# A new two-dimensional FFT (radix-4/2 over d, 128-point transforms over s, a t transform with ±f unpacking) under a scheduler with buffer pools

## The chip, the cores and the metric

The kernel runs on one core of a Trainium2 chip. Times are device microseconds (us) of one execution, and medians over several. Most executions agree within a per cent (in b1's batch, 9 of the 11 of the unchanged kernel lay within 1% of their median). A run is marked slow when it lies more than 1.5% above the fastest of the same kernel. "Span" is the profiled length of one execution, about 2 us shorter than its time. Engines: PE is TensorE (PEld its weight loads), DVE VectorE, ACT ScalarE, POOL GpSimd, SP SyncE, which issues most transfers. Nothing here uses more than one core.

## The reference, cut to what matters

Two paths read the same x (2048 rows s, 512 columns d) and are mixed by a gate for each row.

```python
def _A_ref(x, w_r, w_i):                       # x: 1 x 2048 x 512
    X = rfft2(x.astype(float32), axes=(-2, -1))    # 2048 x 257, complex
    X = X * (w_r + 1j * w_i)
    return irfft2(X, s=(S, D)).astype(bfloat16)
def _B_ref(x, w1, b1, w2):
    h = einsum("bsd,df->bsf", x, w1) + b1          # 512 -> 1792
    act = h * tanh(softplus(h))
    return einsum("bsf,fd->bsd", act, w2)
g = sigmoid((x * gate_w).sum(-1, keepdims=True))
return g * _A_ref(...) + (1 - g) * _B_ref(...)
```

## The kernel before

Both FFT directions are written as matmuls with constant matrices: a transform over d (a1), one over part of s (s1), a round trip through DRAM scratch that turns the data so that the rest of s lies on the partitions, a second transform there (s2), the multiplication by W, and the same way back (s2i, scratch, s1i, a1i). The two large matmuls of path B (mm1 and mm2) fill TensorE's gaps. A list scheduler orders all tasks on each engine before the kernel is emitted.

The d transform makes half-width products (64 output partitions each), 16 matmuls of 256 columns for each of the 16 tiles:

```python
def f_a1(e, t=t, bank=bank):
    for bx in range(2):
        for dt_ in range(4):
            for c in range(2):
                ins = e.matmul(ps[64 * c:64 * c + 64, bank, 256 * bx:256 * (bx + 1)],
                               xT[:, dt_, t, bx:128:2],
                               FD_sb[:, dt_, 256 * c:256 * (c + 1)], ...)
```

The result of s1 is evicted (copied by ACT or DVE out of ps, TensorE's output in PSUM) into one of **two** staging tiles, each stored to scratch after four tiles; the third group of four waits for the first store:

```python
T2 = sb("T2", [128, 2, 4, 512], BF)
Y1s = [T2[:, i, :, :].rearrange("p g (h k) -> p (g h) k", h=2) for i in range(2)]
...
def f_e2(e, t=t, sbank=sbank):
    return e.activation(Y1s[(t // 4) % 2][:, (t % 4)::4, :], ps[:, sbank, :]..., AF.Copy)
if t % 4 == 3:
    ...dma(f"r1w{gi}_{bx}", scr1_w[:, b0:b0 + 4, :], Y1s[gi % 2][:, 4 * bx:4 * bx + 4, :], ...)
```

W is loaded by GpSimd's queue, one transfer for the real and one for the imaginary part. Each row is read twice, so that each transfer fills all 128 partitions with 16,448 contiguous bytes:

```python
Wrv = A_w_r.rearrange("(j g) k -> j (g k)", g=32).unsqueeze(1).to_broadcast([64, 2, 32 * 257])
t_wr = dma("ld_wr", WaT[:].rearrange("p g k -> p (g k)"), Wrv, ..., queue="pool", deps=t_w1)
```

Of the kernel before, what the change touches and what calls it, by code (L numbers as in the profile page):

```python
# [8 lines left out]
BF = mybir.dt.bfloat16  # L9
# [5 lines left out]
NT = 16  # L15
NFT = 14
NCH = 4

# [8 lines left out]
def _q_of(c, e):  # L27
    return 64 * c + e


def _build_consts():
    cs = {}
    d = np.arange(D, dtype=np.float64)[:, None]
    k = np.arange(256, dtype=np.float64)[None, :]
    ang = 2 * np.pi * d * k / D
    FD = np.zeros((D, 512))
    FD[:, :256] = np.cos(ang)
    FD[:, 256:] = -np.sin(ang)
    FD[:, 256] = (-1.0) ** np.arange(D)
    cs["FD"] = FD.reshape(4, 128, 512).transpose(1, 0, 2)  # L40
    n = np.arange(D, dtype=np.float64)[None, :]
    kk = np.arange(256, dtype=np.float64)[:, None]
    ang2 = 2 * np.pi * kk * n / D
    GD = np.zeros((512, D))
    GD[:256, :] = 2 * np.cos(ang2)
    GD[256:, :] = -2 * np.sin(ang2)
    GD[0, :] = 1.0
    GD[256, :] = (-1.0) ** np.arange(D)
    GD /= (S * D)
    cs["GD"] = GD.reshape(2, 2, 128, D).transpose(2, 1, 0, 3).reshape(128, 4, D)  # L50
    a = np.arange(64, dtype=np.float64)[:, None]
    e = np.arange(64, dtype=np.float64)[None, :]
    qre = np.array([_q_of(0, ee) for ee in range(64)])
    qim = np.array([_q_of(1, ee) for ee in range(64)])
    M1 = np.zeros((128, 32, 128))
    G1 = np.zeros((128, 32, 128))
    for b in range(32):
        th = -2 * np.pi * e * (32 * a + b) / S
        c_, s_ = np.cos(th), np.sin(th)
        M1[0:64, b, qre] = c_  # L60
        M1[64:128, b, qre] = -s_
        M1[0:64, b, qim] = s_
        M1[64:128, b, qim] = c_
        thi = (2 * np.pi * e * (32 * a + b) / S).T
        ci, si = np.cos(thi), np.sin(thi)
        G1[qre, b, 0:64] = ci
        G1[qim, b, 0:64] = -si
        G1[qre, b, 64:128] = si
        G1[qim, b, 64:128] = ci
    cs["M1"] = M1  # L70
    cs["G1"] = G1
    RF = np.zeros((128, 128))
    RI1 = np.zeros((128, 128))
    for b in range(32):
        for dd in range(32):
            ph = -2 * np.pi * b * dd / 32
            fw = [[np.cos(ph), np.sin(ph)], [-np.sin(ph), np.cos(ph)]]
            iv = [[np.cos(ph), -np.sin(ph)], [np.sin(ph), np.cos(ph)]]
            for m2 in range(2):
                for ci_ in range(2):  # L80
                    for co in range(2):
                        RF[4 * b + 2 * ci_ + m2, 4 * dd + 2 * m2 + co] = fw[ci_][co]
                        RI1[4 * dd + 2 * m2 + co, 4 * b + 2 * ci_ + m2] = iv[co][ci_]
    RI2 = RI1[np.arange(128) ^ 1, :]
    P1k = np.zeros((128, 128))
    P0k = np.zeros((128, 128))
    Jm = np.zeros((128, 128))
    for dd in range(32):
        for m2 in range(2):
            for co in range(2):  # L90
                po = 4 * dd + 2 * m2 + co
                P1k[4 * (31 - dd) + 2 * (1 - m2) + co, po] = 1
                if m2 == 1:
                    P0k[4 * (31 - dd) + 2 + co, po] = 1
                else:
                    P0k[4 * ((32 - dd) % 32) + co, po] = 1
                Jm[po ^ 1, po] = 1
    small = np.stack([RF, RI1, RI2, P0k, P1k, Jm], axis=1)
    cs["SMALL"] = small
    cs["SGN"] = np.where(np.arange(128) % 2 == 0, 1.0, -1.0).astype(np.float32).reshape(128, 1)  # L100
    return cs


class _Task:
    __slots__ = ("name", "eng", "dur", "fn", "deps", "lat", "sem", "semval", "idx", "sig",
                 "start", "done", "succ", "bl", "prio", "xfer", "ninst", "opts", "isdma")

    def __init__(self, name, eng, dur, fn, lat=0.0, prio=0.0):
        self.name = name
        self.eng = eng  # L110
        self.dur = dur
        self.fn = fn
        self.deps = []
        self.lat = lat
        self.sem = None
        self.semval = 0
        self.idx = -1
        self.sig = 0
        self.start = 0.0
        self.done = 0.0  # L120
        self.succ = []
        self.bl = 0.0
        self.prio = prio
        self.xfer = 0.0
        self.ninst = 0
        self.opts = None
        self.isdma = False


OPT_BIAS = {"act": 0.0}  # L130
SCH = dict(eps=0.1, sync=0.1)


class _Cnt:
    def __init__(self, e):
        self._e = e
        self.n = 0

    def __getattr__(self, k):
        f = getattr(self._e, k)  # L140

        def w(*a, **kw):
            self.n += 1
            return f(*a, **kw)  # L144

        return w


class _Graph:
    ENGS = ("pe", "act", "dve", "pool", "sp")  # L150

    def __init__(self):
        self.tasks = []
        self.last_w = {}
        self.readers = {}
        self.cur_prio = 0.0
        self.win_first = None
        self.win_last = None

    def add(self, name, eng, dur, fn, reads=(), writes=(), lat=0.0, deps=(), prio=None):  # L160
        if prio is None:
            prio = self.cur_prio
        t = _Task(name, eng, dur, fn, lat, prio)
        dset = []
        seen = set()

        def _add(d):
            if d is not None and d is not t and id(d) not in seen:
                seen.add(id(d))
                dset.append(d)  # L170

        for d in deps:
            _add(d)
        for r in reads:
            _add(self.last_w.get(r))
        for w in writes:
            _add(self.last_w.get(w))
            for rd in self.readers.get(w, ()):
                _add(rd)
        for r in reads:  # L180
            self.readers.setdefault(r, []).append(t)
        for w in writes:
            self.readers[w] = []
            self.last_w[w] = t
        t.deps = dset
        t.idx = len(self.tasks)
        self.tasks.append(t)
        return t

    def add_multi(self, name, opts, reads=(), writes=(), deps=(), prio=None):  # L190
        e0, d0, f0 = opts[0]
        t = self.add(name, e0, min(o[1] for o in opts), f0, reads=reads, writes=writes, deps=deps, prio=prio)
        t.opts = list(opts)
        return t

    def schedule(self):
        tasks = self.tasks
        for t in tasks:
            t.succ = []
            t.start = -1.0  # L200
# [3 lines left out]
        for t in reversed(tasks):  # L204
            m = 0.0
            for s_ in t.succ:
                if s_.bl > m:
                    m = s_.bl
            t.bl = t.dur + t.lat + m
        nleft = {id(t): len(t.deps) for t in tasks}  # L210
        ready = [t for t in tasks if not t.deps]
        free = {e: 0.0 for e in self.ENGS}
        order = {e: [] for e in self.ENGS}
        nsched = 0
        EPS = SCH['eps']
        SYNC_LAT = SCH['sync']
        dq_free = 0.0
        dq2_free = 0.0
        while nsched < len(tasks):
            best = None  # L220
            best_est = None
            ests = []
            for t in ready:
                if t.opts is None:
                    est = free[t.eng]
                    for d in t.deps:
                        dd = d.done + (0.0 if d.eng == t.eng else SYNC_LAT)
                        if dd > est:
                            est = dd
                else:  # L230
                    bo = None
                    for (oe, od, of) in t.opts:
                        e_ = free[oe]
                        for d in t.deps:
                            dd = d.done + (0.0 if d.eng == oe else SYNC_LAT)
                            if dd > e_:
                                e_ = dd
                        sc = e_ + od + (OPT_BIAS.get(oe, 0.0) if (self.win_first is not None and self.win_first.start >= 0 and self.win_last.start < 0) else 0.0)
                        if bo is None or sc < bo[0] - 1e-9:
                            bo = (sc, e_, oe, od, of)  # L240
                    est = bo[1]
                    t.eng, t.dur, t.fn = bo[2], bo[3], bo[4]
                ests.append((est, t))
                if best_est is None or est < best_est:
                    best_est = est
            best = None
# [666 lines left out]
```

## Time and profile before

The first three runs had a median of 179.32 us (177.5 to 179.56).

| From the profile before (span 176.1 us) | us |
|---|---|
| TensorE busy | 156.0 |
| of it mm1 and mm2 | 53.1 + 50.2 |
| of it the d transform forward (a1), back (a1i) | 18.6, 15.3 |
| longest idle stretch of TensorE (from 32.6 us) | 8.9 |
| stage t (s2, W, s2i) starts | 73.4 |
| from TensorE's last matmul to the end | 5.6 |

These lines are from the page of the kernel before: busy time and share of each engine, then the span in 40 equal slices (a digit is the busy share in tenths, PEclk the granted TensorE clock in tenths, GB/s what the transfers moved).

```profile
span 176.1 us, 2584 instructions
PE 156.0 (89%) x1032; PEld 78.8 (45%) x1047; DVE 67.2 (38%) x117; ACT 67.1 (38%) x112; POOL 19.3 (11%) x47
...
PE   1798997405999999999999999999999999999990
...
PEclk9999999975999999999999999999999999999997
DMA  5999199993003594800113020286013010101101
GB/s 170 298 415 387 30 323 433 370 381 108 4 0 117 174 280 135 372 0 0 58 63 123 0 119 4 119 270 207 0 64 116 4 60 0 63 0 60 51 9 60
```

TensorE is nearly full except in the first slices and in a hole from the eighth to the tenth. Just before and in it (slices seven to nine) the transfers run at 370 to 433 GB/s.

The groups of instructions, by line, engine, operation and tiles (busy us, mean ns; then idle time just before and what ended it), and the transfers (KB each, median us to landing):

```profile
L144 PE MATMUL ps<-fdgd,xT 128*64 128x256 bf16 x256 | 18.6, 294 | 1.3 <-DMA fdgd<-c_fd 1.2
L144 ACT ACTIVATE T<-ps 128x512 bf16<-128x512 f32 x13 | 7.7, 598 | 16.6 <-DMA scr<-T 10.1
...
WaT<-in_A_w_r_dram POOLq DMA_DIRECT2D x1, 2056.0 KB, 8.7
WbT<-in_A_w_i_dram POOLq DMA_DIRECT2D x1, 2056.0 KB, 13.3
```

The hole is explained by the second line: ACT waits 10.1 us for the store of a staging tile, and TensorE for ACT. The view of the chain that ended last shows the store, and the timeline of TensorE the hole (start, length, instruction, and in brackets the idle time before it):

```profile
21.74 18.41 DMA scr<-T
...
41.49 8.76 PE L144 MATMUL ps<-xT,w_sb 128*128 128x512 bf16 x31 [8.88 <-ACT hsreg L144]
```

**Two modes.** In later batches two executions of this unchanged kernel took 167.0 and 167.3 us at a mean granted clock of 0.999. The other 40 of 42 took 176.8 to 182.9. All profiles of it are of the longer kind. Where one of the two stood in a batch, its neighbours near 180 us were marked slow by the 1.5% rule, so I don't use the ratios of those two batches and compare medians of the changed kernels instead.

### The profile page before, as it was taken

Reading aid. Unit: us, or ns where it says so; the run is one execution under the profiler, and the core shown is the slowest. Engines: PE = TensorE matmul, PEld = TensorE weight load, DVE = VectorE, ACT = ScalarE, POOL = GpSimd, SP = SyncE. Lnnn points to the kernel's source line nnn. Section 1 sums busy time; section 2 is a strip of 40 time slices with the busy share of each in tenths; the row PEclk is TensorE's granted clock in tenths of the full one; section 3 lists DMA queues with packets and bytes.
Section 4 is the critical chain, followed back from the end, with each engine's and each line's share of the span. In section 5 each row is a group of like instructions: output and inputs, shape, how many; then the busy total and the mean of one; then the engine's idle time right before and its main releaser. Section 6 shows DMA issues by size and latency. Waiting matters only on the chain.

```text
span 176.1 us, 2584 instructions
## 1 busy us (share of the span) xinstructions
PE 156.0 (89%) x1032; PEld 78.8 (45%) x1047; DVE 67.2 (38%) x117; ACT 67.1 (38%) x112; POOL 19.3 (11%) x47
## 2 busy tenths in 40 slices
PE   1798997405999999999999999999999999999990
PEld 0676673202367433344444444435555554444440
DVE  0133523000015300245577877400856635160624
ACT  2154637006674677668442186163311230300000
POOL 1000250099100040012000000000000000000000
PEclk9999999975999999999999999999999999999997
DMA  5999199993003594800113020286013010101101
GB/s 170 298 415 387 30 323 433 370 381 108 4 0 117 174 280 135 372 0 0 58 63 123 0 119 4 119 270 207 0 64 116 4 60 0 63 0 60 51 9 60
DMA packets 13856, 23.97 MB, mean 136 GB/s; under 512 B 853, under 2 KB 10325, under 8 KB 13077
## 3 DMA queue, kind: packets, MB, share of 16 engines
q1 hardware_dynamic: 13076, 17.77, 29.3%
q0 software_dynamic: 768, 6.05, 8.7%
q8 instruction: 8, 0.13, 0.3%
q14 instruction: 4, 0.02, 0.1%
HBM read 17.52 MB, written 6.29 MB: 135 GB/s over the span
## 4 chain that ended last, share of the span: by engine, by line
PE 80%; DMA 13%; DVE 3%; issue 1%; SPq 1%; ACT 1%; ACTq 0%
PE ps L144 80%; DMA scr<-T 10%; DMA hsreg<-in_A_x_dram 3%; DVE bs L144 2%; DVE xT L144 1%; SPq L144 1%; DVE T L144 0%; ACT T L144 0%; ACT hsreg L144 0%; ACTq L831 0%; SPq L831 0%
## 5 line engine op out<-in xcount | busy, mean ns | idle before, releaser
L144 PE MATMUL ps<-xT,w_sb 128*128 128x512 bf16 x218 | 53.1, 388 | 10.4 <-ACT hsreg L144 10.0
L144 PE MATMUL ps<-w_sb,hsreg 128*128 128x512 bf16 x216 | 50.2, 379 | 0.4
L144 ACT ACTIVATE hsreg<-ps,b1f 128x512 bf16<-128x512 f32 x56 | 38.1, 688 | 22.2 <-PE ps L144 22.0
L144 PEld LDWEIGHTS ps<-xT,w_sb 128*128 128x128 bf16 x224 | 19.6, 99 | 39.6 <-ACT hsreg L144 20.4
L144 PEld LDWEIGHTS ps<-w_sb,hsreg 128*128 128x128 bf16 x224 | 21.6, 98 | 24.6
L144 DVE CAST T<-ps 128x512 bf16<-128x512 f32 x19 | 13.0, 691 | 37.5 <-PE ps L144 37.3
L144 DVE TENSOR_SCALAR bs<-ps,omg 128x512 bf16<-128x512 f32 x15 | 11.3, 751 | 29.7 <-PE ps L144 21.5
L144 PE MATMUL ps<-fdgd,xT 128*64 128x256 bf16 x256 | 18.6, 294 | 1.3 <-DMA fdgd<-c_fd 1.2
L144 ACT ACTIVATE TT<-ps 128x256 bf16<-128x256 f32 x18 | 6.9, 452 | 25.3 <-PE ps L144 25.2
L144 PEld LDWEIGHTS ps<-fdgd,xT 128*64 128x64 bf16 x256 | 14.0, 117 | 4.5 <-issue 1.9
L144 DVE TENSOR_TENSOR bs<-ps,WaT 128x512 bf16<-128x512 f32 x16 | 10.3, 685 | 13.5 <-PE ps L144 13.5
L144 ACT ACTIVATE Abuf<-ps 128x512 bf16<-128x512 f32 x16 | 9.6, 598 | 15.3 <-PE ps L144 15.3
L144 PE MATMUL ps<-fdgd,TT 128*128 128x512 bf16 x64 | 15.3, 379 | 0.0
L144 ACT ACTIVATE T<-ps 128x512 bf16<-128x512 f32 x13 | 7.7, 598 | 16.6 <-DMA scr<-T 10.1
L144 DVE SCALAR_TENSOR_TENSOR bs<-ps,gcol,bs 128x512 bf16<-128x512 f32 x16 | 12.0, 751 | 3.7 <-PE ps L144 2.8
L144 DVE COPY xT<-ps 128x512 bf16<-128x512 bf16 x13 | 5.3, 423 | 14.4 <-PE ps L144 14.4
L144 DVE TENSOR_TENSOR bs<-ps,WbT 128x512 bf16<-128x512 f32 x16 | 10.2, 682 | 0.0
L144 PEld LDWEIGHTS ps<-fdgd,TT 128*128 128x128 bf16 x64 | 6.3, 98 | 7.6
L144 PE MATMUL ps<-identt,hsreg 128*128 128x128 bf16 x64 | 6.0, 238 | 3.9 <-DMA hsreg<-in_A_x_dram 3.4
L144 PE MATMUL ps<-bs,sm 128*128 128x512 bf16 x32 | 8.4, 379 | 0.0
L144 POOL TENSOR_SCALAR WbT<-WbT,sgnf 128x8224 bf16<-128x8224 bf16 x1 | 7.1, 7122 | 0.1
L144 PEld LDWEIGHTS ps<-identt,hsreg 128*128 128x128 bf16 x64 | 4.1, 106 | 5.9 <-DMA hsreg<-in_A_x_dram 3.8
(53 smaller groups left out, 57.1 us busy)
## 6 DMA issues: line engine op xcount, KB each, us to landing
WaT<-in_A_w_r_dram POOLq DMA_DIRECT2D x1, 2056.0 KB, 8.7
WbT<-in_A_w_i_dram POOLq DMA_DIRECT2D x1, 2056.0 KB, 13.3
scr<-T SPq DMA_DIRECT2D x8, 256.0 KB, 8.8
Abuf<-scr SPq DMA_DIRECT2D x2, 1024.0 KB, 5.9
scr<-T SPq DMA_DIRECT2D x4, 512.0 KB, 2.6
Abuf<-scr SPq DMA_DIRECT2D x4, 512.0 KB, 5.4
out_dram<-bs SPq DMA_DIRECT2D x8, 256.0 KB, 2.0
w_sb<-in_B_w_dram SPq DMA_DIRECT2D x2, 896.0 KB, 12.3
```

Of the source, the lines that this page charges most:

```text
L144: return f(*a, **kw)
```

## The change

The intent: less TensorE work in the FFT, no waits on shared staging, and one scheduler that also gives out buffers. The d transform becomes a radix-4/2 step: additions and subtractions on DVE and GpSimd first, then matmuls of full width. The way back makes half the columns and unfolds them in the last element-wise step. All 16 staged tiles have their own place. The t transform unpacks frequencies +f and −f together, for which the mirrored half of W has to lie on partitions 32 to 63 and 96 to 127 in reverse order. So W is loaded in pieces: 32 neighbouring partitions in long rows, and 16 partitions (every second one) in 514-byte rows written backward. They go on SP's queue, among the scratch stores. PSUM banks and small tiles come from pools at scheduling time. The whole diff is some 1,600 lines; its core (cuts marked):

```diff
-                for bx in range(2):
-                    for dt_ in range(4):
-                        for c in range(2):
-                            ins = e.matmul(ps[64 * c:64 * c + 64, bank, 256 * bx:256 * (bx + 1)], ...)
+                ff = mk("d", XB[:, 2:4, tr_, :], xT[:, 0:2, tr_, :], xT[:, 2:4, tr_, :], ALU.subtract)
+                ff = mk("s", xss, xT[:, 0:2, tr_, :], xT[:, 2:4, tr_, :], ALU.add)
+                ...  # two more of half the size
+                e.matmul(o[:, :, 2:4, :], XB[:, 2, t, :], f4(256), start=True, stop=False)
+                e.matmul(o[:, :, 2:4, :], XB[:, 3, t, :], f4(512), start=False, stop=True)
+                e.matmul(o[:, :, 0, :], XB[:, 0, t, :], f2(0), start=True, stop=True)
+                return e.matmul(o[:, :, 1, :], XB[:, 1, t, :], f2(128), start=True, stop=True)
 ...
-        T2 = sb("T2", [128, 2, 4, 512], BF)
+        A1s = R4[:].rearrange("p (t k) -> p t k", t=NT)
 ...
-        t_wr = dma("ld_wr", WaT[:].rearrange("p g k -> p (g k)"), Wrv, ..., queue="pool", deps=t_w1)
+                v = src_t.rearrange("(g h e2 j) k -> g h e2 j k", g=16, h=2, e2=2)
+                wl.append(dma(f"ld_{nm}p{co}", dst[base:base + 32, :, :].rearrange("p j k -> p (j k)"),
+                              v[:, 0, :, :, :].rearrange("g e2 j k -> g e2 (j k)"), 32 * 16448, ...))
+                nb = dst[base + 32:base + 64, :, :]
+                def back(part, j, npart, nj, pstep):
+                    return bass.AP(nb.tensor, nb.offset + part * row + j * 257, [[pstep * row, npart], [-257, nj], [1, 257]])
+                n1 = bass.AP(src_t.tensor, src_t.offset + 65 * 257, [[128 * 257, 16], [257, 32], [1, 257]])
+                wl.append(dma(f"ld_{nm}r{co}", back(0, 31, 16, 32, 2), n1, 16 * 32 * 514, ...))
+                ...  # 31 more such rows for the odd partitions, and one row for each of 16 partitions
 ...
+        fpool = _Pool(4)
+        mpool = _Pool(4)
```

Here `base` is 0 or 64. W's bytes don't change (4.2 MB).

## The prediction

> **What bounds the kernel now.** The chain that ended last is 80% TensorE and 13% DMA; TensorE is busy 156.0 of 176.1 us (page, parts 1 and 4). The timeline of TensorE shows its 20 us of idle time: 3.0 at the start, 8.9 at 32.6-41.5 us (waiting for ACT, which itself waited 10.1 us to reuse the staging tile T, whose store had an 18.4 us DMA piece in the chain), 5.6 after the last matmul, small gaps elsewhere. The kernel is bound by TensorE work plus one DMA stall. DVE and ACT (38% each) have slack on average.
>
> **What the change removes on TensorE.** (groups by shape)
> - d transform forward: 256 half-width matmuls of 256 columns, 18.6 us, become per tile two of 256 and two of 128 columns at full width. Estimate from s1 (5.5 us/32 at 256 columns, part of it overlap; about 0.11-0.12 each) and s1i (4.9/64 at 128 columns): about 6 us. Saves 12.5.
> - d transform back: 64 matmuls of 512 columns, 15.3 us, become 64 of 256: about 7.5. Saves 7.8.
> - s and t matmuls, mm1 (53.1) and mm2 (50.2) stay. TensorE falls to about 134-136 us.
>
> **What it adds or moves.**
> - Butterflies: 32 SBUF add/subtracts (23 on DVE, 9 on GpSimd by the order listing). [...]
> - Front stage: 16 transposes plus 32 full evictions (0.60 ACT, 0.69 DVE) plus butterflies make about 18 us on ACT and 21 on DVE. The front becomes eviction-bound: it should end near 29 us (the first transform now ends at 57.6).
> - All 16 staged tiles have their own place, so the 8.9 us stall goes.
> - W weights: the same 4.1 MB, now hardware queue, half of it in 514-byte rows, queued among scratch writes. About 11.8 MB precede the scratch reads; at the 370 GB/s of the busy slices that lands near 34 us, so stage t starts at about 39-41 us (now 73.4).
> - Stage t: each gp has four 256-wide multiplies instead of two 512-wide. The 256-wide casts start 0.335 us apart, the 512-wide multiplies 0.60: 1.28 becomes about 1.5 us per gp, 26-29 us with its share of evictions. TensorE has about 31 us there. Near balance: 32-34 us.
> - Final stage: DVE gets three instructions a tile (0.75 + 2x0.45) instead of one; still about 26 us under 36 us of TensorE work. The end is 8 last output adds hidden under mm2, tail about 3.3 us instead of 5.6.
>
> **Sum.** Front and its wait to 40; stage t to 73; mm2/mm1 filler 9 us while scratch 2 goes round, to 82; remaining TensorE work (64 s1i, 64 a1i, 92 mm1, 168 mm2) 69 us plus 1-2 of waits, to 152.5; tail to 156 span. Run time is 2 us above the span here. Prediction 157.5 us, range 151 to 167 (from 179.3). Faster 0.95, same 0.03, slower 0.02.
>
> **What would show it right.** TensorE busy 133-138 us; a1 group 5-7 us, a1i 7-8; no gap over 4 us after about 32 us; idle time concentrated before 40 us; the chain's DMA share falling, DVE/ACT share rising in the front; 256-wide multiplies at 0.42-0.45 us.
>
> **What would make it wrong.** 514-byte rows slow, so that W and scratch reads land after 45 us; the front's in-order DVE/ACT/GpSimd waits stretching it past 34 us, with TensorE's granted clock dropping in the gaps (0.975 mean now; the first stage already ran at half speed: 1.92 against 1.07 us a tile); strided W reads or self-waits making stage t DVE-bound (over 36 us).

The sum of the forecast is a span of 156 us, a time of 157.5 (range 151 to 167). The sum itself starts at 40 us, where the transfers put stage t's start, and comes to 157.5.

## The result, and the profile after

The changed kernel took 168.0 us median (166.5 to 169.2, four runs, one of them marked slow) against 179.4 (177.5 to 179.8, four runs). The ratio of the fast runs is 0.935, 95% interval 0.924 to 0.946: faster, but by 11 us where 22 were predicted, and just outside the range. A ratio here is the mean time of one kernel's fast runs over that of the other's of the same rounds, so it isn't quite the ratio of the medians. Repeated on another chip, the changed kernel took 168.3 us (r1 below).

The page of the changed kernel, the same parts:

```profile
span 164.8 us, 2256 instructions
PE 137.2 (83%) x835; PEld 72.3 (44%) x850; DVE 74.5 (45%) x172; ACT 76.4 (46%) x126; POOL 9.3 (6%) x16
...
PE   1397998693002999999999999999999999999991
...
PEclk9999999999655699999999999999999999999999
DMA  4798999999999993030303891100101000011011
GB/s 144 282 374 336 248 157 342 153 280 139 344 135 282 385 354 118 38 127 0 127 0 142 242 258 64 64 4 0 64 0 66 4 0 0 0 64 64 4 64 64
...
L687 PE MATMUL ps<-Wa,SM 128*128 128x32 bf16 x1 | 0.2, 217 | 13.9 <-DMA Wb<-in_A_w_i_dram 13.9
...
L851 PE MATMUL ps<-GD,TT 128*128 128x256 bf16 x64 | 9.1, 273 | 0.0
...
Wa<-in_A_w_r_dram SPq DMA_DIRECT2D x2, 514.0 KB, 9.5
Wb<-in_A_w_i_dram SPq DMA_DIRECT2D x2, 514.0 KB, 11.2
```

TensorE's work fell by 18.8 us (156.0 to 137.2), nearly as predicted (20 to 22). The span fell by 11.3 only, because TensorE's idle time (span less busy) rose from 20.1 to 27.6 us. The old 8.9 us hole is gone and a new one of 13.9 us stands in slices 10 to 13. A transfer ended it: the first matmul that reads W (L687, which prepares a small table) waited for W's imaginary part. The GB/s line shows what differs: in the fifth to thirteenth slices it swings between about 140 and 340, while the DMA digits say 9. The engines read as busy and move little.

The timeline of TensorE around the hole:

```profile
28.49 0.82 PE L637 MATMUL ps<-R,FT 128*128 128x512 bf16 x2 [0.36 <-ACT R L505]
30.70 7.94 PE L785 MATMUL ps<-xT,w_sb 128*128 128x512 bf16 x36 [1.39 <-ACT hsb L793]
52.54 0.22 PE L687 MATMUL ps<-Wa,SM 128*128 128x32 bf16 x1 [13.89 <-DMA Wb<-in_A_w_i_dram]
...
53.21 0.39 PE L733 MATMUL ps<-R,SM 128*128 128x256 bf16 x1 [0.19 <-DMA R<-scr]
```

The front ends at 29.3 us, as predicted; TensorE then takes the mm1 work that fits, and stands still from 38.6 to 52.5. Stage t starts at 53.2 instead of the predicted 39 to 41. SP's queue shows why the scratch reads (R<-scr) came as late as W:

```profile
20.34 7.72 SPq L480 DMA_DIRECT2D Wa<-in_A_w_r_dram  x4
28.23 0.47 SPq L480 DMA_DIRECT2D scr<-R  x1
28.74 6.41 SPq L480 DMA_DIRECT2D Wb<-in_A_w_i_dram  x4
35.68 0.34 SPq L480 DMA_DIRECT2D FT<-c_gt  x1
36.18 0.36 SPq L480 DMA_DIRECT2D scr<-R  x1
36.59 7.71 SPq L480 DMA_DIRECT2D Wb<-in_A_w_i_dram  x4
45.83 1.81 SPq L480 DMA_DIRECT2D R<-scr  x4
```

To issue four W pieces took SP 6.4 to 7.7 us here, and 3.3 us for the first four, at 15.84; what held SP is not shown. The last scratch store was issued at 36.18, and the reads that wait for it only at 45.83: the store, behind three quarters of W, took 9.57 us. The chain that ended last has both (start, length):

```profile
36.18 9.57 DMA scr<-R
45.83 7.33 DMA R<-scr
```

The table by stretches (us from:to and length; busy us of PE, PEld, DVE, ACT, POOL; granted clock; DMA share; GB/s), changed kernel:

```profile
29.30:38.60 9.30, 7.91 (x37) 3.45 (x36) 0.99 (x3) 8.31 (x13) 0.00 (x0) 1.00 1.08 194
38.60:52.50 13.90, 0.04 (x1) 0.00 (x0) 0.00 (x0) 0.69 (x1) 0.00 (x0) 0.64 1.15 221
52.50:85.90 33.40, 32.80 (x158) 15.24 (x163) 24.69 (x72) 17.45 (x29) 0.00 (x0) 0.95 0.42 155
85.90:161.50 75.60, 75.12 (x420) 38.63 (x427) 29.10 (x56) 31.75 (x51) 0.00 (x0) 1.00 0.19 60
```

Between 29.3 and 52.5 us the transfers ran at 194 and 221 GB/s with a share above 1. After the hole, all went as predicted or slightly better. So the question is narrow: why do 4.2 MB of W, which the kernel before loaded without TensorE waiting for it, take so long here?

### The profile page after: what moved, and what is told of

Same layout as the page of the kernel before. It is cut to its first block, busy times and chain, and to the rows that moved or that the text cites. A ratio compares the mean times of both kernels' runs of the same rounds, so it can differ in the third digit from the quotient of the medians.

```text
span 164.8 us, 2256 instructions
## 1 busy us (share of the span) xinstructions
PE 137.2 (83%) x835; PEld 72.3 (44%) x850; DVE 74.5 (45%) x172; ACT 76.4 (46%) x126; POOL 9.3 (6%) x16
## 3 DMA queue, kind: packets, MB, share of 16 engines
HBM read 16.34 MB, written 6.29 MB: 137 GB/s over the span
## 4 chain that ended last, share of the span: by engine, by line
PE 76%; DMA 13%; ACT 4%; POOL 2%; issue 1%; SPq 1%; DVE 0%; POOLq 0%
PE ps L803 29%; PE ps L785 28%; DMA scr<-R 6%; DMA R<-scr 4%; PE ps L851 4%; DMA R<-in_A_x_dram 3%; PE ps L832 2%; PE ps L759 2%; PE ps L760 2%; PE ps L735 2%; PE ps L582 2%; ACT R L505 2%; POOL PX L602 1%; PE ps L659 1%; PE ps L637 1%
## 5 line engine op out<-in xcount | busy, mean ns | idle before, releaser
L793 ACT ACTIVATE hsb<-ps,b1f 128x512 bf16<-128x512 f32 x56 | 37.9, 688 | 30.5 <-PE ps L785 30.1
L803 PE MATMUL ps<-w_sb,hsb 128*128 128x512 bf16 x218 | 49.7, 379 | 0.3
L803 PEld LDWEIGHTS ps<-w_sb,hsb 128*128 128x128 bf16 x224 | 21.8, 98 | 25.5
L505 ACT ACTIVATE R<-ps 128x512 bf16<-128x512 f32 (+1 forms) x29 | 16.8, 594 | 7.7 <-PE ps L760 5.0
L504 DVE CAST R<-ps 128x512 bf16<-128x512 f32 (+1 forms) x19 | 12.8, 689 | 9.1 <-PE ps L760 6.2
L746 DVE TENSOR_TENSOR PX<-ps,Wa 128x256 bf16<-128x256 f32 x32 | 12.0, 416 | 0.6 <-PE ps L734 0.6
L746 DVE TENSOR_TENSOR PX<-ps,Wb 128x256 bf16<-128x256 f32 x32 | 12.0, 417 | 0.1
L687 PE MATMUL ps<-Wa,SM 128*128 128x32 bf16 x1 | 0.2, 217 | 13.9 <-DMA Wb<-in_A_w_i_dram 13.9
L851 PE MATMUL ps<-GD,TT 128*128 128x256 bf16 x64 | 9.1, 273 | 0.0
L874 DVE SCALAR_TENSOR_TENSOR R<-ps,gcol,PX 128x256 bf16<-128x256 f32 x16 | 7.7, 482 | 1.2 <-ACT PX L865 0.8
L875 DVE SCALAR_TENSOR_TENSOR R<-ps,ngcol,PX 128x256 bf16<-128x256 f32 x16 | 7.6, 476 | 0.0
## 6 DMA issues: line engine op xcount, KB each, us to landing
w_sb<-in_B_w_dram SPq DMA_DIRECT2D x4, 896.0 KB, 11.8
```

What stands on the lines that cost most here:

```text
L504: G.add(name, [("dve", dve_dur(n), lambda e: e.tensor_copy(out=outf(), in_=inf())), ("act", act_dur(n), lambda e: e.activation(outf(), inf ...
L505: ("act", act_dur(n), lambda e: e.activation(outf(), inf(), AF.Copy))],
L746: ins = e.tensor_tensor(out=po, in0=px, in1=pw, op=ALU.mult)
L793: return e.activation(hsb[:, hb, ft, :], ps[:, bk(sl), :], AF.Mish, bias=b1f[:, ft:ft + 1])
L803: ins = e.matmul(ps[:, bk(sl), :], hsb[:, hb, ft, 128 * tl:128 * (tl + 1)], w2_sb[:, ft, :], start=(ft == 0), stop=(ft == NFT - 1))
L851: ins = e.matmul(ps[:, bk(sy), 256 * hh:256 * (hh + 1)], TT[:, st.i, i, :], GD[:, i, :], start=(i % 2 == 0), stop=(i % 2 == 1))
```

## The experiments

Three theories. **Rows:** half of W now goes in 514-byte rows, slow each. **Queue order:** W stands between the scratch stores on SP's queue; on another queue it would not hold them up. **Spread:** a transfer to few partitions (narrowness), or to partitions that lie close together, is slow whatever its rows. The change's W pieces all lie within 0 to 63 or 64 to 127, where those of the kernel before filled all 128. Twelve kernels ran.

### m1: the row shapes by themselves

A kernel that only loads, two transfers of each kind and a wait (its result is wrong).

```diff
+ a: rows(16 partitions, every 2nd of 32..63) x 32 rows of 514 B, backward     # the kernel's own
+ c: 512 B of each row, rows 514 B apart in SBUF;  d: 512 B rows 512 B apart in SBUF
+ h: 16 partitions as in a, 16448 B contiguous;    i: 32 neighbours x 16448 B
+ j: 128 partitions x 2056 B contiguous;           k: as a, but 16 neighbouring partitions
```

> Measures the disputed cost by itself (the result is wrong on purpose): fourteen kinds of load into SBUF, each two transfers of about 263 KB in one queue, one kind after the other with a wait between. The mirrored half of a weight in the changed kernel goes as 16 partitions x 32 backward rows of 514 B, and the trace shows about 140 GB/s while they run. Row theory (short rows of 514 B are what is slow): 514 B rows take about 1.9 us per 263 KB more than the fixed time wherever they go (16 or 128 partitions, forward or backward), 16 KB rows into the same 16 partitions about 0.7 us. Narrowness theory (few partitions are what is slow): 16 KB rows into 16 or 32 partitions are as slow as 514 B rows, and 514 B rows into 128 partitions are fast. [...]

It ran once, 89.5 us. From one kind's issue to the next's: a 6.22, c 6.06, d 4.82, h 4.74, i 7.12, j 3.34, k 9.86 us. All moved 0.53 MB except i, 1.05 MB. Part of each is fixed: 128 full partitions took 3.34 us for 0.53 MB here and 4.72 for 1.05 MB in m2, so I estimate 1.96 us fixed and 1.38 us per 0.53 MB. Less that, short rows cost 4.26 us against 2.78 in the same 16 partitions (a against h, a factor of 1.5), and those 16 partitions cost 2.78 against 1.38 of all 128 (h against j, a factor of 2). With k, 16 neighbours, the short rows were slower again: 7.9 us. Rows matter, and so does which partitions they go to, which the rows theory has no place for. The direction and the place of the rows in the source mattered little (forward rows 6.05 us against a's 6.22; d, with its source rows 514 bytes apart, 4.82, and with source rows 1,024 bytes apart 4.75). In these 16 partitions the 512-byte rows of d are about as fast as the long rows of h (4.82 against 4.74 us), while the same rows laid 514 bytes apart (c) took 6.06, so there the place of the rows in SBUF cost more than their length. Less the fixed part, d gains a factor of 1.5 over a (4.26 to 2.86 us).

Two more kinds of this run speak against narrowness alone: 514-byte rows spread over all 128 partitions, four to each (f), took 5.42 us, and 512-byte rows laid 512 bytes apart and spread so (g) 4.30, against j's 3.34. Less the fixed part, f costs 3.46 us against j's 1.38: short rows stay slow on all partitions, and spreading them gained less (4.26 to 3.46) than spreading long ones.

### e1: long rows, same partitions

```diff
-                n1 = bass.AP(src_t.tensor, ..., [[128 * 257, 16], [257, 32], [1, 257]])
-                wl.append(dma(f"ld_{nm}r{co}", back(0, 31, 16, 32, 2), n1, ...
+                lrow = lambda part, ln: bass.AP(nb.tensor, nb.offset + part * row, [[2 * row, 16], [1, ln]])
+                n1 = bass.AP(src_t.tensor, ..., [[128 * 257, 16], [1, 32 * 257]])
+                wl.append(dma(f"ld_{nm}r{co}", lrow(0, 32 * 257), n1, ...
```

The mirrored half is no longer mirrored, so the result is wrong; bytes, partitions and engine order stay.

> The changed kernel with the mirrored half of both weights loaded forward in rows of 16 KB into the same 16 partitions, by the same number of transfers at the same place in the queue (wrong result on purpose; the instruction order of every engine is the same). Row theory: 2.07 MB at about 390 instead of 140 GB/s saves about 9.4 us of DMA time ahead of the scratch reads; the 13.9 us wait of TensorE before the first table matmul shrinks to about 4 us, time about 158 us (156 to 161). Narrowness theory and queue-order theory (scratch transfers held back behind the weights in one queue, whatever their rows): 166 to 168 us, no change.

163.0 us (162.2 to 163.5, four fast runs). The wait before the table's matmul fell to 10.2 us:

```profile
PE ps L687 <- DMA Wb<-in_A_w_i_dram: 10.2, 1, 10.2
```

The row theory expected about 158. It got 5 us of the 10: rows are a part, not the main cause.

### e2: W on another queue

```diff
                 wl.append(dma(f"ld_{nm}p{co}", ...,
-                              writes=[(o, co, 0)], deps=wdep))
+                              writes=[(o, co, 0)], deps=wdep, queue="pool"))
```

and the same for the other three pieces; the result is right.

> The changed kernel with the 16 weight loads, rows unchanged, issued from the GpSimd queue, so that scratch stores and reads no longer stand behind them in the SyncE queue; all instructions of TensorE, ACT and DVE in the same order. Queue-order theory: the fourth scratch store is issued at about 30.5 us instead of 36.2, its reads land near 42, time falls by 6 to 10 us (158 to 162). Row theory: the DMA engines are full until 52 us whichever queue feeds them, the last weight still lands near 50, time 165 to 169.

170.7 us (170.5 to 172.3, four fast runs): no faster than the changed kernel, if anything slower (1.6%, from another batch). The waits of TensorE show the trade:

```profile
PE ps L687 <- DMA Wb<-in_A_w_i_dram: 8.4, 1, 8.4
...
PE ps L733 <- DMA R<-scr: 7.6, 1, 7.6
```

W came earlier, the scratch reads later, and the sum of the two (16.0 us) is worse than 13.9 + 0.2. Order only chose who waits. W was no faster by this queue: in slices 6 to 11 of this run's page the transfers move 176 to 206 GB/s while the DMA digits say 9. The queue theory falls.

### f1: a first repair, long rows and a reversal on chip

The mirrored half lands in long rows in a staging tile, and DVE and GpSimd copy it in reverse order.

```diff
+        Wst = hsb[:, 1:3, :, :]...                      # mm1's output buffer, still unused
+        lrow = lambda part, ln: bass.AP(nb.tensor, ..., [[2 * row, 16], [1, ln]])
+        def f_rev(e, ...): return e.tensor_copy(out=dst[base + 32:base + 64, ...], in_=nb[:, 31 - 16 * hh:...:-1, :])
+        G.add(f"rev_{nm}{co}{hh}", [("dve", REV_DVE, f_rev), ("pool", REV_POOL, f_rev)], ...)
```

> A repair with the right result: the mirrored halves are loaded forward in 16 KB rows into the still unused part of the activation buffer, and DVE and GpSimd, which idle from 30 to 52 us, copy them with the rows reversed (eight copies of 32 x 4112 elements; at GpSimd's 0.87 ns an element of the first kernel about 3.7 us each[...]). Row theory: time 156 to 162, better than both kernels, stage t starting near 40 to 44 us. Queue-order and narrowness theories: 166 us or more.

163.5 us (162.7 to 164.5, four fast runs), right, and no better than e1: its last reversing copies could only start at 49.9 us, when the last staging transfer had landed. It also made a new wait. The timelines of GpSimd and DVE:

```profile
27.58 7.43 POOL L574 COPY Wa<-hsb 32x4112 bf16<-32x4112 bf16 x2 [4.05 <-DMA hsb<-in_A_w_r_dram]
```

```profile
27.63 3.91 DVE L609 TENSOR_TENSOR R<-PX 128x256 bf16<-128x256 bf16 x2
...
35.16 1.24 DVE L574 COPY Wa<-hsb 32x4112 bf16<-32x4112 bf16 x1
```

A copy took 1.24 us on DVE and 3.6 to 4.7 on GpSimd, and while GpSimd copied, two DVE additions that take 0.31 us each in the changed kernel took 3.91 together. Why is not shown; the later repairs use DVE alone.

### m2: the partitions by themselves

```diff
+ a: 128 partitions x 4112 B        b: 64 neighbours x 8224 B     c: every 2nd of 128, 64 x 8224 B
+ d: 32 neighbours x 16448 B        e: every 2nd of 64, 32        f: every 4th of 128, 32 x 16448 B
+ g: 16 neighbours x 16448 B        h: every 8th of 128, 16 x 16448 B
+ i..l: every 4th, 32 x 32 rows of 514 B, 514/528/544/576 B apart
```

> The transfers by themselves again, now two of 526 KB per kind (wrong result on purpose). In the first such run 16 neighbouring partitions moved 66 GB/s and 16 alternate ones 136 with the same 514 B rows, and 32 neighbouring partitions with 16 KB rows about 206 against about 390 for 128 partitions. [...] 64 neighbouring partitions are no faster than 32 (about 206 GB/s), 32 alternate partitions of the first 64 the same, every fourth of 128 partitions fast (350 or more), 64 alternate ones of 128 fast, 16 neighbours about 105, every eighth about 206. Partition-count theory: speed follows the number of partitions: 64 twice 32, every fourth as slow as 32 neighbours. [...]

Issues of SP, start and length; what matters is the distance from one start to the next. Shown are the starts of a, b and c, then of f and g:

```profile
9.02 0.85 SPq L40 DMA_DIRECT2D dst<-in_A_w_r_dram  x2
13.74 1.14 SPq L42 DMA_DIRECT2D dst<-in_A_w_r_dram  x2
21.00 1.13 SPq L44 DMA_DIRECT2D dst<-in_A_w_r_dram  x2
...
40.37 1.12 SPq L50 DMA_DIRECT2D dst<-in_A_w_r_dram  x2
45.67 0.78 SPq L52 DMA_DIRECT2D dst<-in_A_w_r_dram  x2
```

| kind | partitions | us | GB/s (estimate, 1.96 us taken off) |
|---|---|---|---|
| a | 128 | 4.72 | 381 |
| c | every 2nd, 64 | 5.06 | 340 |
| f | every 4th, 32 | 5.30 | 315 |
| b | 64 neighbours | 7.26 | 199 |
| d | 32 neighbours | 6.99 | 209 |
| e | every 2nd of 64, 32 | 7.32 | 196 |
| h (half the bytes) | every 8th, 16 | 4.68 | 193 |
| g (half the bytes) | 16 neighbours | 6.71 | 111 |

The number of partitions does not decide: 32 spread ones (f, 315 GB/s) are faster than 64 neighbours (b, 199). The rates fall into three groups: all, every second and every fourth of the 128 partitions run at 315 to 381 GB/s; 64 or 32 neighbours, every second of 64 and every eighth of 128 at 193 to 209; 16 neighbours at 111. So within the first 64 partitions, 64 gave no more than 32 (b and d), and over all 128 every fourth sufficed for most of the rate, though f stayed below the 350 expected, while every eighth (h) did not suffice. Why the groups lie so is not shown. The short rows i to l, on every fourth of 128 partitions, took 6.12 to 6.29 us at every spacing, about 250 GB/s, against about 123 for m1's kind a in 16 of 32 partitions (0.53 MB in 4.26 us). So a wider spacing did not help. Spread alone doesn't set the rate of short rows: m1's f, on all 128 partitions, makes only about 152 (0.53 MB in 3.46 us), which stays unexplained. This ran once, 95.7 us, with a wrong result.

### e3: the same bytes to all partitions

```diff
-                wl.append(dma(f"ld_{nm}p{co}", dst[base:base + 32, :, :]..., 32 * 16448, ...
-                ... (the pieces r, n, s)
+                for i, (nr, ch) in enumerate(((8, "p"), (4, "r"), (3, "n"), (1, "s"))):
+                    sv = bass.AP(src_t.tensor, ..., [[32 * 257, 64], [0, 2], [1, nr * 257]])
+                    wl.append(dma(f"ld_{nm}{ch}{co}", dst[:, r0:r0 + nr, :]..., sv, 128 * nr * 514, ...
```

As many transfers and bytes, the order of every engine unchanged; the result is wrong.

> The changed kernel with the same number of weight transfers of the same bytes in the same places of the queue, but each to all 128 partitions with rows of 0.5 to 4 KB (wrong result on purpose; order on every engine unchanged). [...] 4.2 MB at about 370 GB/s instead of about 165 saves about 13 us of DMA time: the wait before the table matmul falls from 13.9 us to under 2, time 154 to 158 us. If the queue's order or the total of bytes were the cause: 161 us or more, as with long rows alone (163.0).

156.1 us (155.4 to 157.3, four fast runs). The wait and the same stretches:

```profile
PE ps L687 <- DMA Wb<-in_A_w_i_dram: 1.8, 1, 1.8
```

```profile
29.30:38.60 9.30, 7.91 (x37) 3.44 (x36) 1.11 (x3) 8.41 (x13) 0.00 (x0) 1.00 1.03 363
38.60:52.50 13.90, 10.81 (x52) 5.04 (x53) 6.85 (x22) 5.08 (x9) 0.00 (x0) 0.75 0.92 307
```

The rate from 29.3 to 38.6 us rose from 194 to 363 GB/s at about the same DMA share (1.08 and 1.03), and the kernel became 11.9 us faster. The spread theory's expectation holds (154 to 158 us). e3 alone changes spread, number of partitions and row length together, and reads each source row twice, as the kernel before did. m2 tells these apart for the transfers: 64 neighbouring partitions gained nothing over 32 (b, 199 GB/s, against d, 209), and its kind a, which reads every byte once, still ran at 381 GB/s.

### e4: all partitions, short rows

```diff
+            for i, (nr, ch) in enumerate(((8, "p"), (4, "r"), (3, "n"), (1, "s"))):
+                dv = bass.AP(dst..., [[row, 128], [-257, nr], [1, 257]])
+                sv = bass.AP(src_t.tensor, ..., [[15 * 257, 128], [257, nr], [1, 257]])
```

Here all of W, not only half, goes in 514-byte rows, backward (wrong), so it overstates the rows' part.

> The changed kernel with its W loads spread over all 128 partitions, but the mirrored half still in 514-byte rows, backward. Result wrong on purpose. It completes a table of two by two: narrow and short 168.0, narrow and long 163.0, wide and long 156.1 us. [...] most of the gain of wide stays, 158 to 161 us, the wait before the first tab matmul 3 to 6 us. Rows theory [...]: 164 us or more.

159.5 us (159.0 to 160.8, four fast runs); the wait is 4.9 us:

```profile
PE ps L687 <- DMA Wb<-in_A_w_i_dram: 4.9, 1, 4.9
```

| median us | 514-byte rows | long rows |
|---|---|---|
| pieces within 64 partitions | 168.0 (half of W short) | 163.0 |
| all 128 partitions | 159.5 (all of W short) | 156.1 |

Spreading saves at least 8.5 us with short rows and 6.9 with long ones; lengthening saves 5.0 within 64 partitions, and 3.4 on all 128 although twice as much of W was short there. Both together make the 11.9 us between the corners, and spread weighs more than rows. The four come from three batches, and the long rows of e3 are 0.5 to 4 KB where those of e1 have 16 KB, so a us more or less means little.

### f3 and f4: repairs that keep the result

In f3 only partitions 0 to 63 of W are loaded, once, in long rows. DVE reverses the mirrored half out of a staging tile and copies 0–63 to 64–127. That halves the bytes instead of widening the transfer. In f4 a constant that isn't needed until later (GT) also moves behind the scratch reads.

```diff
+        def wcopy(nm, dst, nb, o, st):
+            f_rev = lambda e: e.tensor_copy(out=dst[32:64, :, :], in_=nb[:, ::-1, :])
+            f_dup = lambda e: e.tensor_copy(out=dst[64:128, :, :], in_=dst[0:64, :, :])
-                wload(*((("wr", Wa, A_w_r, "Wa"), ("wi", Wb, A_w_i, "Wb"))[t // 8]), (t // 4) % 2, ...)
+                if t < 8:
+                    wload(*((("wr", Wa, A_w_r, "Wa", 32), ("wi", Wb, A_w_i, "Wb", 96))[t // 4]), ...)
 # f4 only:
-        dma("ld_gt", GT[:], ..., deps=t_s1)                  # before the scratch reads
+        dma("ld_gt", GT[:], ..., deps=t_s1 + t_r1w)          # after them
```

> Repair, right result: only the first 64 partitions of each weight come by DMA (2.1 instead of 4.2 MB, long rows), DVE reverses the mirrored half and copies partitions 0-63 to 64-127 while it idles after 30 us (a 32 x 4112 reversing copy on DVE took 1.23 us, so about 2.5 us each, four of them). [...] about 11 instead of 25 us of DMA time for the weights, stage t starts near 40 us, time 154 to 158. GpSimd, whose copies held DVE back in the first repair, has none here.

> The same with the 0.5 MB constant GT, which nothing needs before 90 us, issued after the scratch reads instead of ahead of the last scratch store. If the front is still bound by DMA time this gives another 1.4 us (about 153 to 156); if not, nothing.

f3: 154.8 us (154.3 to 156.5, five runs). f4: 153.3 us (152.5 to 153.7, four runs), both with the right result. f4 beats the kernel before by about 26 us and the changed one by 14.7 (medians). Its gain over f3, 1.5 us, is one per cent; the runs of the two, from one batch, do not overlap. Its page and its timeline at the place of the hole:

```profile
PE 136.7 (90%) x835; PEld 72.1 (48%) x850; DVE 84.2 (56%) x176; ACT 76.4 (50%) x126; POOL 9.1 (6%) x16
```

```profile
31.45 8.81 PE L792 MATMUL ps<-xT,w_sb 128*128 128x512 bf16 x39 [1.39 <-ACT hsb L800]
41.12 0.28 PE L740 MATMUL ps<-R,SM 128*128 128x256 bf16 x1 [0.86 <-DMA R<-scr]
```

Stage t starts at 41.1 us. The four copies cost DVE 9.2 us, at a time when it had nothing else to do.

### b1 and b2: the kernel before, again and with four staging tiles

b1 is the kernel before unchanged. b2 gives it four staging tiles instead of two:

```diff
+        Y1x = sb("Y1x", [128, 2, 4, 512], BF)
-        Y1s = [T2[:, i, :, :].rearrange(...) for i in range(2)]
+        Y1s = [b_[:, i, :, :].rearrange(...) for b_ in (T2, Y1x) for i in range(2)]
```

> The kernel before, unchanged. In the two batches so far most of its executions took 177 to 183 us, and one in each took 167. If it has two modes, five rounds should show mostly 177 to 181 us and perhaps one or two near 167; if the 167s were accidents of the first batch positions, all stay at 177 to 181 us.

> The kernel before with four staging tiles for the scratch instead of two, so that no eviction waits for an earlier scratch store (the 8.9 us stall of the profile before). If that stall is what the slow mode of before consists of: 167 to 171 us in all executions, TensorE idle before the last shear-stage work of the front down from 8.9 to under 2 us. If the mode has another cause: still 177 to 180 us in most.

b1: 180.1 us (179.1 to 181.0, six fast runs); the 167 us mode didn't show, and its other eleven runs of that batch took 176.8 to 181.0. The ratio of b1 to these is 1.010 [1.004, 1.017] though the kernels are the same, so a per cent means nothing here. b2: 168.4 us (167.6 to 170.8, four runs, the 170.8 marked slow), right, ratio 0.944 [0.936, 0.951]. Its page and timeline:

```profile
PE 155.0 (93%) x1032; PEld 78.6 (47%) x1047; DVE 67.3 (40%) x117; ACT 67.3 (40%) x112; POOL 19.3 (12%) x47
```

```profile
32.93 7.35 PE L144 MATMUL ps<-xT,w_sb 128*128 128x512 bf16 x31
```

The hole of 8.9 us is gone. So the kernel before lost 10.4 us (178.9 to 168.4) to having two staging tiles. b2's clock of 1.0 and its time are those of the two odd executions, which fits that they were executions without this stall; as none of them was profiled, that stays open. The lesson is sharper than the mode: two more staging tiles in the old kernel bring it to 168.4 us, as fast as the whole new FFT, whose 18.8 us of saved matmuls its own W load paid back.

### r1: the changed kernel again

Unchanged, on another chip.

> The changed kernel, unchanged, on another chip and in another batch, since the experiments were compared with its four first runs. If chip and batch play no part: 166 to 170 us, with the wait of about 14 us before the first tab matmul. If they do: outside that range, and the comparisons across batches have to be read with that much care.

168.3 us (166.6 to 169.7, four runs, one marked slow), ratio 0.937 [0.925, 0.948], and the wait before L687 was 14.8 us. So comparisons across batches hold to about a per cent.

## Why the prediction was wrong

- **TensorE's work: right.** Predicted 134 to 136 us busy, measured 137.2. The way back was a little worse than estimated (9.1 us against 7.5). The forward transform's four groups sum to 16.8 us in the listing, which would contradict the predicted 6, but their records overlap: on the timeline the four matmuls of one tile start at 24.62 us and those of the next at 24.95, so 16 tiles take about 5.3 us (0.33 each).
- **Front: right in time.** Predicted to end near 29 us, ended at 29.3. That evictions bound it is not shown: from 8 to 29.3 us TensorE was busy for 19.2 us, DVE for 17.6 and ACT for 16.2. The butterflies took DVE 0.31 us on average at 256 columns and 0.48 to 0.56 at 512. Three long ones (1.37, 0.52 and 0.81 us) overlap in time with a butterfly of GpSimd's; the medians are 0.29 and 0.42. The two sizes let one take the fixed cost apart: from 256 to 512 columns a butterfly gets about 0.13 us longer (fastest 0.281 and 0.414), a multiply out of PSUM about 0.27 (0.416 here, 0.682 in the kernel before). So each further column cost a butterfly half of what it cost a multiply out of PSUM, while at 256 columns the whole instruction was faster by a factor of only 1.3 to 1.4 (0.31 on average and 0.29 in the median, against 0.416).
- **The old stall: right.** The 8.9 us hole went, and b2 shows that it was worth 10.4 us.
- **W's load: wrong, and this is the step.** The prediction said: "About 11.8 MB precede the scratch reads; at the 370 GB/s of the busy slices that lands near 34 us, so stage t starts at about 39-41 us (now 73.4)." It started at 53.2 us, 13 us late. The amount was right, the rate was not: 11.6 MB had moved when SP issued the reads at 45.8 us, 254 GB/s on average. The 370 GB/s were read off slices in which the W of the kernel before filled all 128 partitions. W's new pieces go to 32 neighbouring partitions, in long rows, or to every second one of 32, in short rows; m1 and m2 put the first at about 206 GB/s (m1's i, m2's d) and the second at about 123 (m1's a), less the fixed part. An estimate from m1: 2.1 MB at 5.16 us per 1.05 MB and 2.1 MB at 4.26 us per 0.53 MB make 27 us, against 11 at the rate of kind j. The 16 us more are of the size of the new 13.9 us wait. e3 shows it in the kernel: the same bytes to all partitions took 156.1 us, and stage t started at 42.1. That this is within 1.4 us of the prediction is partly luck, as the 2.1 us by which stage t still starts late are made up later (last points).
- **The named risk: half right.** "514-byte rows slow" stood among what could go wrong, and the late landing it named (after 45 us) came true. But rows alone (e1) were 5.0 of the 11.9 us that e3 gained.
- **Stage t: right.** Predicted 32 to 34 us, measured 32.7 (53.2 to 85.9). The 256-wide multiplies took 0.416 us, predicted 0.42 to 0.45. The low clock after the hole (0.95 from 52.5 to 85.9) made it no slower than predicted.
- **The rest: slightly better.** From stage t's end to TensorE's end the prediction had 79.5 us (73 to 152.5) and the trace 75.6. The work left was as predicted (from 94.5 us on, 90 matmuls of mm1 and 163 of mm2 in the trace, 92 and 168 in the prediction; over the span it lists 220 and 218 matmuls beside 224 weight loads each, so a few records are missing). It took 67.0 us without waits instead of 69 and 1 to 2 of waits, and the filler before it 8.6 instead of 9. The tail was 3.3 us, as predicted.
- **The sum.** +13.2 us at stage t's start, −0.3 in stage t, −3.9 after it and −0.2 in the tail make the 8.8 us by which the span of 164.8 misses the 156 of the prediction's text.

## What to carry to other kernels

Cost a load by the partitions its destination touches, and not by its bytes and row length alone: a rate read from 128-partition transfers did not hold for a piece of 32 or 64 neighbouring partitions (381 GB/s in m2's a, 209 and 199 in d and b). A DMA share near 1 with half the usual GB/s was a mark of it here (1.08 and 1.15 at 194 and 221 GB/s in the changed kernel, 1.03 at 363 in e3), though not of it alone: m1's short rows (a) show a share of 1.25 at 139 GB/s (from 11.75 to 13.25 us). Here, issuing from another queue did not help (170.7 us against 168.0); spreading the destination did (156.1, with a wrong result), and so did moving fewer bytes and copying on an idle engine (154.8). And before a large rewrite, take away the largest single stall: here two more staging tiles were worth as much as the new algorithm with its first W load.
